# Gate and val products of the last two batches by seven block products in place of eight, with Silu on ScalarE and the weight sums on GpSimd

## The chip, the cores and the metric

One core of one Trainium2 chip. The metric is the device time of an execution in microseconds, the median of some runs. Before: 407.11 us (three runs, 406.99 to 408.16).

## The reference

Sigmoid attention for 8 batches of 12 heads, 448 positions, 64 per head, and behind it a gated block with two weight matrices in and one out:

```python
scores = scale * np.matmul(q, k.transpose(0, 1, 3, 2)) - np.log(S)
attn = 1.0 / (1.0 + np.exp(-scores))
x = matmul(attn, v), heads side by side: 3584 tokens x 768
g = x @ w_gate                       # 768 x 1536
silu = g * (1.0 / (1.0 + np.exp(-g)))
val = x @ w_val                      # 768 x 1536
out = silu * val @ w_out             # 1536 x 768
```

Inputs and output are float32; the kernel multiplies in bf16 (scores) and fp16 (the rest) and accumulates in float32.

## The kernel before, in words

**Stages.** Attention runs in 24 steps of four heads (`QB` = 3 steps per batch). In a step q, k and v are loaded to staging tiles on the SP queue, cast to 16 bits (mostly on GpSimd, L270), q and k transposed (first by TensorE, then by DMA, L410). `burst` (L417) makes the scores of one of seven key slots in two banks of PSUM, four 64x64 matmuls of 448 columns; ACT applies the sigmoid and writes `pt` (L448). `pv` (L455) multiplies with v; DVE or ACT copy the result to `xT` (L268, L266), fp16, features on partitions, tokens along the row: six tiles of 128x448 per batch.

**Gate and val.** `f1(b, f)` (L529) does two blocks f and f+1 of 128 hidden features of one batch. For each block gate takes six 128x128 products (over the 768 inputs) into one bank, val the same. Each 128x128 product is issued as four 64x64 quarters (`quarters`, L511), in two halves; between the halves of one bank pair, a nop on ACT (`turn`, L500, L504) keeps two row halves from writing the same bank at once. Then ACT makes the sigmoid of gate (L546), DVE multiplies it with gate (L552) and, when val is there, that with val (L559) into `hT`, 1024 times too large. Two batches share one `hT`.

**Output.** `f2_set(m, k)` (L631) multiplies two token tiles of a pair m of batches with `w_out`. It takes two tiles (e, o) and two halves of features, a 2x2 block product, and does it by seven block products in place of eight: sums of `hT` blocks on DVE (L661, L664, L667, L734), sums of `w_out` blocks made once on DVE (L605), seven products of six matmuls, and adds on DVE and ACT that put the parts together (L687, L727). In `f2_pair` (L757) two products go side by side as quarters; `f2_single` (L788) does one with whole 128x128 matmuls (L678). The last 64 rows of tile 6 of an even m are kept by two GpSimd copies (`keep`, L620, L623). Stores go out through GpSimd (L697, tiles `osb`, three of them), or, in the final part (`final`), through SP and ACT (staging memory, `osf`, four).

**Order.** The body does not issue instructions at once. Each `op` (L255) notes its engine, a duration by the author, what it depends on and which ring slots it takes and gives back. The loop at L872 queues ops step by step: per step and quarter (`sl`) a scores burst, gate/val work by a due count `nf` (L880), and output items whenever `f2acc` (grown by 12.5/22 per quarter, L919) allows. `list_schedule` (L70) then plays this through with the noted durations and fixes the order of each engine's queue. The engines run their queues in that order and wait only on semaphores. A tag in `FREE` (before: the eight PSUM banks `P`) takes any free slot, others go round a ring.

**Staging memory.** `stage` has eleven tiles. The first five (`NEARLY`) stay staging to the end and hold the final `osf`; the other six hold the sums of `w_out` and the kept rows from the middle of the run.

Of the kernel before, what the change touches and what calls it, by code (L numbers as in the profile page):

```python
# [9 lines left out]
FP32 = mybir.dt.float32  # L10
FP16 = mybir.dt.float16
BF16 = mybir.dt.bfloat16
COPY = mybir.ActivationFunctionType.Copy
SIGM = mybir.ActivationFunctionType.Sigmoid
MULT = mybir.AluOpType.mult
ADD = mybir.AluOpType.add
SUB = mybir.AluOpType.subtract
# [10 lines left out]
class Op:  # L28
# [3 lines left out]
    def __init__(self, eng, dur, fn, deps=(), mode=("F", "F"), take=(), give=(), desc=(0, 0)):  # L32
        self.eng, self.dur, self.fn, self.mode = eng, dur, fn, mode
        self.deps = [d if isinstance(d, tuple) else (d, 0.0) for d in deps if d is not None]
        self.take = [Slot(t) for t in take]
        self.give = list(give)
        self.rank = self.t0 = self.t1 = None
        self.first = False
        n, size = desc
        self.hold = n == 1792  # L40
        self.dma = 2.0 if n == 1792 else n / 16 * max(0.042, size / 22300 - 0.003)
# [13 lines left out]
LAG = 1  # L55
# [8 lines left out]
TURN = "ACT"  # L64
WO = 4
MARGIN = 1.0
FREE = {"P"}


def list_schedule(ops, bufs, window):  # L70
# [113 lines left out]
def kernel(  # L184
# [10 lines left out]
    nc = tc.nc  # L195

    B, H, S, D = q.shape
    DM = H * D
    DFF = moe_w_gate.shape[1]
    KC = DM // 128  # L200
# [14 lines left out]
    ctx.enter_context(tc.manual_schedule())  # L215

    slots = {"A": 2, "P": 8, "st": 11, "src": 2,
             "v16": 3, "qkT": 3, "pt": 10, "xT": 14, "osb": 3, "osf": 4, "S": 2, "t1": 3, "s16": 2}

    idn = one.tile([128, 128], BF16, tag="idn", name="idn")  # L220
    sb_t = one.tile([128, 1], FP32, tag="sbiast", name="sbiast")
# [33 lines left out]
    def op(*a, **kw):  # L255
        o = Op(*a, **kw)
        ops.append(o)
        return o

    def bank(name, n=0):  # L260

        return psum.tile([128, 512], FP32, tag=f"P{R['now'].got('P')[n].n}", bufs=1, name=name)

    def cp(eng, o, i):
        if eng == "ACT":
# [7 lines left out]
    T = {}  # L273
# [169 lines left out]
    def sig(key, dep, slot):  # L443
        def fn(a):
            def go():
                if a == 0:
                    T[("pt",) + key] = sb.tile([128, 2, S], FP16, tag="pt", bufs=slots["pt"], name="pt")
                nc.scalar.activation(out=T[("pt",) + key][:, a], in_=T[("sc",) + key][a][:, 0:S], func=SIGM, bias=sbias,  # L448
                                     scale=qkscale)
            return go  # L450
        x = op("ACT", 0.44, fn(0), deps=[dep], take=["pt"], give=slot[1:2])
        R["pt ring", key] = x.take
        R["sig"] = R[("pt",) + key] = op("ACT", 0.44, fn(1), deps=[x and (x, LAT["ACT"] + LATE)], give=slot[:1] + slot[2:])

    def pv(i):  # L455

# [72 lines left out]
    def f1(b, f):  # L529

        two = (f, f + 1)
        m, o = divmod(b, 2)

        def both(w, nm, parts, p):
            def fn():
                if p == 0:
                    for n, x in enumerate(two):
                        T[nm, b, x] = bank("ps_" + nm, n)[:, 0:S]
                quarters([[(T[nm, b, x], w[x // FC][:, j, (x % FC) * 128:(x % FC + 1) * 128], T["xT", b, j]) for x in two]
                          for j in range(*parts[p][1:])], parts, p, (nm, b, f))  # L540
            return fn

        def fs(f):
            def fn():
                t = T["s16", b, f] = sb.tile([128, S], FP16, tag="s16", bufs=slots["s16"], name="s16")
                nc.scalar.activation(out=t, in_=T["g", b, f], func=SIGM)  # L546
            return fn

        def ft(f):
            def fn():  # L550
                t = T["t1", b, f] = sb.tile([128, S], FP16, tag="t1", bufs=slots["t1"], name="t1")
                nc.vector.tensor_tensor(out=t, in0=T["g", b, f], in1=T["s16", b, f], op=MULT)  # L552
            return fn

        def fh(f):
            def fn():
                if o == 0 and f == 0:
                    T["hT", m] = sb.tile([128, NF, 2 * S], FP16, tag="hT", bufs=2, name=f"hT_{m}")
                nc.vector.scalar_tensor_tensor(  # L559
                    out=T["hT", m][:, f, o * S:(o + 1) * S], in0=T["v", b, f], scalar=HSC,  # L560
                    in1=T["t1", b, f], op0=MULT, op1=MULT)
            return fn
        xs = [(R["xT", b, j], 0.19 * j) for j in range(KC)]
        old = R["f2", m - 2] if m >= 2 and b % 2 == 0 else []

        def joint(w, nm, deps):
            a = None
            parts = [(0, 0, KC), (1, 0, KC)]
            if (b, f) == (0, 0) and nm in SPLIT:
                parts = [(0, 0, 4), (1, 0, 4), (1, 4, KC), (0, 4, KC)]  # L570
            ws = [(x, 0.38 * n) for c in {x // FC for x in two} for n, x in enumerate(R["w16", "w" + nm, c])]
            for p, (t, j0, j1) in enumerate(parts):
                same = p and parts[p - 1][0] == t
                a = op("PE", 0.19 * (j1 - j0), both(w, nm, parts, p), mode=("Q", "Q"), take=[] if p else ["P", "P"],
                       deps=[(x, 0.19 * n) for n, (x, _) in enumerate(xs[j0:j1])] + deps + ws +
                       [a and ((a, LAT["PE"] + LATE) if same else turn(a, (nm, b, f, p - 1)))])
                banks = banks if p else a.take
            return a, banks
        g, gbank = joint(wg16, "g", [])
        ts = []  # L580
        for n, x in enumerate(two):
            s = op("ACT", 0.45, fs(x), deps=[g], take=["s16"])
            s.first = 2
            ts.append(op("DVE", 0.54, ft(x), deps=[s], take=["t1"], give=s.take + gbank[n:n + 1]))

        def val():
            v, vbank = joint(wv16, "v", old + [(g, 1.0)])
            if f == NF - 2:
                v.give += [x for o, _ in xs for x in o.take]
            for n, (x, t) in enumerate(zip(two, ts)):  # L590
                R["hT", b, x] = op("DVE", 0.54, fh(x), deps=[v, t] + old, give=vbank[n:n + 1] + t.take)
        return val

    def weight_sums():

# [276 lines left out]
    for i in range(NQ + QB + 2):  # L872
        att = i < NQ
        for sl in range(4):
            if i < QB:
                nf = 0
            elif i < QB + 4:
                nf = 1 if sl < 3 else 0
            else:
                nf = min(2, max(0, 4 * (i - QB) + sl - LAG - fpos + 1))  # L880
            if i < NCW and sl == 3:
                cast_wc(i)
            if WO < i <= WO + 4 and sl == 1:
                for f in range(3 * (i - WO - 1), 3 * (i - WO)):
                    cast_wo(f)
            if i > WO + 5 or i == WO + 5 and sl > 1:
                for _ in range(WSN):
                    next(wsums, None)
            f1s = []
            while len(f1s) < nf and fpos < B * NF and ("xT", fpos // NF, KC - 1) in R:  # L890
                f1s.append(divmod(fpos, NF))
                fpos += 1
            later = bursts(i, sl)
            for ds in later[:1 if i >= SPREAD else 2]:
                burst(ds)
            if sl == 0 and QB < i <= NQ:
                pv(i - 1)
            if sl == 0 and 0 < i < QB:
                pv(i - 1)
            if sl == 3 and i == QB - 1:  # L900
                pv(i)
            if att and i + 1 < NPE and sl in (1, 2):
                tr_pe(i + 1, sl - 1)
            for b, f in f1s:
                f1_step(b, f)
            for ds in later[1:] if i >= SPREAD else []:
                burst(ds)
            if att and sl == 0 and i + 2 < NQ:
                casts(i + 2)
            if att and sl == 1 and NPE <= i + 2 < NQ:  # L910
                tr_dma(i + 2)
            if sl == 1:
                if AHEAD <= i + 3 < NQ:
                    loads(i + 3)
                if WO <= i < WO + 4:
                    for f in range(3 * (i - WO), 3 * (i - WO + 1)):
                        load_wo(f)
                    uses[1] = uses[0]
            f2acc = f2acc + 12.5 / 22.0 if f2q else 0.4  # L919
            while f2q and f2acc >= f2q[0][0] and ("ws", 4, NH - 2) in R:  # L920
                w, fn = f2q.pop(0)
                f2acc -= w
                fn(not att)
    while fpos < B * NF:
        b, f = divmod(fpos, NF)
        fpos += 1
        f1_step(b, f)
    while f2q:
        f2q.pop(0)[1](True)

    window = {"PE": 40, "ACT": 30, "DVE": 40, "POOL": 8, "SP": 1}
    end = 0.0
# [39 lines left out]
```

## Time and profile before

| | |
|---|---|
| median of the runs | 407.11 us |
| profiled execution, its span | 407.6 us (its own run time is not given apart) |
| TensorE busy (matmuls) | 400.1 us, 7871 instructions shown |
| VectorE (DVE) busy | 230.0 us, 420 |
| ScalarE (ACT) busy | 223.2 us, 472 |
| GpSimd (POOL) busy | 132.7 us, 194 |
| HBM read and written | 47.19 and 11.01 MB, 143 GB/s over the span |
| chain that ended last, by line | gate and val L522 54%, output L522 and L678 24%, scores 8%, pv 7% |

The profile is of one execution. Busy time of TensorE is modelled at the ends, as matmuls are pipelined: a 64x64 matmul of 448 columns is listed with 349 ns, although the next one starts long before its end. To see how fast TensorE goes, one divides a stretch of the chain by its matmuls. "PEld" are weight loads, which run beside matmuls. A line such as L522 is a helper that both gate/val and output products go through, so its groups are told apart by the tiles they write: `ps_g`, `ps_v` and `ps_o`. The chain follows the work that ended last from the end back to the start: its pieces, in order of time, have no room between them when an engine is what bounds the kernel.

### The profile page before, as it was taken

To read this page: it belongs to the slowest core of one execution; us is meant where nothing else is said; L and a number is where in the kernel's file an instruction comes from. 1 tells how busy PE (TensorE), PEld (TensorE's weight loads), DVE (VectorE), ACT (ScalarE), POOL (GpSimd) and SP (SyncE) were. 2 spreads that over 40 slices of the span, in tenths; PEclk is the share of its full clock that TensorE was granted. 3 is DMA by queue.
4 is the path that set the end of the run, shared out by engine and by line. 5 is a ranking of instruction groups with operands and counts; after the bars stand their busy time and mean duration, and the time that the engine had idled before them with its cause. 6 is when DMAs were issued, how large, how long until landed. Compare 5 with 4: busy or idle time off the path is not lost.

```text
span 407.6 us, 17541 instructions
## 1 busy us (share of the span) xinstructions
PE 400.1 (98%) x7871; PEld 306.8 (75%) x7873; DVE 230.0 (56%) x420; ACT 223.2 (55%) x472; POOL 132.7 (33%) x194
## 2 busy tenths in 40 slices
PE   8999999999999999999999999999999999999995
PEld 3446667668998787665679888889989898997663
DVE  2624544447795467553564664745465656546874
ACT  4997677757767743377647456475474552121100
POOL 1888855656454221522332322422310200000000
PEclk9999999999999999999999999999999999999998
DMA  7999999999676609455665564663500303010335
GB/s 268 380 376 376 376 277 318 304 320 264 184 185 183 160 26 203 139 129 108 209 183 92 172 136 143 177 133 122 124 4 3 80 2 77 7 42 18 101 85 148
DMA packets 64795, 67.58 MB, mean 166 GB/s; under 512 B 35536, under 2 KB 60880, under 8 KB 64720
## 3 DMA queue, kind: packets, MB, share of 16 engines
q1 hardware_dynamic: 62864, 59.78, 51.6%
q0 software_dynamic: 1536, 6.29, 6.0%
q8 instruction: 61, 1.00, 1.0%
q10 hardware_dynamic: 320, 0.39, 0.3%
q14 instruction: 14, 0.11, 0.1%
HBM read 47.19 MB, written 11.01 MB: 143 GB/s over the span
## 4 chain that ended last, share of the span: by engine, by line
PE 95%; ACT 2%; DMA 1%; issue 1%; DVE 0%; ACTq 0%
PE ps_v L522 27%; PE ps_g L522 27%; PE ps_o L522 16%; PE ps_sc L427 8%; PE ps_pv L468 7%; PE ps_o L678 7%; ACT pt L448 2%; PE ps_warm L818 1%; PE ps_tr L384 1%; DMA st<-in_q_dram 1%; DVE st L687 0%; DVE src L268 0%; ACTq L504 0%
## 5 line engine op out<-in xcount | busy, mean ns | idle before, releaser
L448 ACT ACTIVATE pt<-ps_sc 128x448 f16<-128x448 f32 x336 | 162.7, 550 | 77.8 <-PE ps_sc L427 77.3
L522 PE MATMUL ps_v<-xT,wv 64*64 64x448 f16 x2304 | 136.2, 349 | 0.0
L522 PE MATMUL ps_g<-xT,wg 64*64 64x448 f16 x2304 | 134.6, 349 | 0.8 <-issue 0.6
L522 PEld LDWEIGHTS <-wg 64*64 64x64 f16 x2304 | 93.7, 107 | 22.2 <-issue 2.4
L522 PEld LDWEIGHTS <-wv 64*64 64x64 f16 x2304 | 93.2, 107 | 21.2 <-issue 1.4
L552 DVE TENSOR_TENSOR t<-ps_g,s 128x448 f16<-128x448 f32 x96 | 56.5, 618 | 71.6 <-ACT s L546 71.6
L546 ACT ACTIVATE s<-ps_g 128x448 f16<-128x448 f32 x96 | 48.1, 545 | 59.0 <-PE ps_g L522 50.0
L559 DVE SCALAR_TENSOR_TENSOR hT<-ps_v,t 128x448 f16<-128x448 f32 x96 | 55.4, 618 | 43.4 <-PE ps_v L522 26.2
L427 PE MATMUL ps_sc<-qkT 64*64 64x448 bf16 x672 | 77.2, 354 | 0.1
L270 POOL CAST src<-st 128x896 bf16<-128x896 f32 (+1 forms) x43 | 40.8, 951 | 64.5 <-DMA st<-in_q_dram 35.8
L270 POOL CAST v<-st 64x448 f16<-64x448 f32 (+1 forms) x72 | 41.5, 577 | 60.0 <-PE ps_pv L468 42.5
L522 PEld LDWEIGHTS <-hT 64*64 64x64 f16 x1080 | 52.2, 107 | 7.0 <-issue 0.2
L522 PE MATMUL ps_o<-wo,hT 64*64 64x384 f16 x648 | 49.2, 323 | 0.0
L522 PE MATMUL ps_o<-st,s 64*64 64x384 f16 x480 | 45.7, 323 | 0.0
L468 PE MATMUL ps_pv<-pt,v 64*64 64x448 f16 x672 | 45.3, 350 | 0.1
L522 PE MATMUL ps_o<-st,hT 64*64 64x384 f16 x432 | 41.2, 323 | 0.0
L427 PEld LDWEIGHTS <-qkT 64*64 64x64 bf16 x672 | 33.7, 107 | 9.9 <-issue 1.6
L687 DVE SCALAR_TENSOR_TENSOR osb<-ps_o,osb 128x384 f32<-128x384 f32 x63 | 32.9, 550 | 10.4 <-PE ps_o L522 6.6
L268 DVE CAST xT<-ps_pv 128x448 f16<-128x448 f32 x40 | 23.6, 617 | 25.0 <-PE ps_pv L468 25.0
L697 POOL DMA_DIRECT2D out_dram<-osb x32 | 16.7, 526 | 59.0 <-DVE osb L687 59.0
L468 PEld LDWEIGHTS <-v 64*64 64x64 f16 x672 | 26.6, 107 | 9.1 <-issue 2.7
L522 PEld LDWEIGHTS <-s 64*64 64x64 f16 x480 | 29.1, 107 | 3.8 <-issue 0.4
(44 smaller groups left out, 212.8 us busy)
## 6 DMA issues: line engine op xcount, KB each, us to landing
st<-in_q_dram SPq DMA_DIRECT2D x24, 448.0 KB, 5.0
st<-in_v_dram SPq DMA_DIRECT2D x24, 448.0 KB, 6.6
st<-in_k_dram SPq DMA_DIRECT2D x23, 448.0 KB, 5.9
out_dram<-osb POOLq DMA_DIRECT2D x32, 192.0 KB, 3.3
st<-in_moe_w_gate_dram SPq DMA_DIRECT2D x12, 384.0 KB, 8.8
st<-in_moe_w_val_dram SPq DMA_DIRECT2D x12, 384.0 KB, 8.8
st<-in_moe_w_out_dram SPq DMA_DIRECT2D x12, 384.0 KB, 7.6
out_dram<-st SPq DMA_DIRECT2D x16, 192.0 KB, 2.8
```

Of the source, the lines that this page charges most:

```text
L268: nc.vector.tensor_copy(out=o, in_=i)
L270: nc.gpsimd.tensor_copy(out=o, in_=i)
L427: nc.tensor.matmul(out=sc[a][64 * (g ^ a):64 * (g ^ a) + 64, 0:S].rearrange("k (s p) -> k s p", s=NS), lhsT=kT[r, s, 64 * g:64 * g + 64], ...
L448: nc.scalar.activation(out=T[("pt",) + key][:, a], in_=T[("sc",) + key][a][:, 0:S], func=SIGM, bias=sbias, scale=qkscale)
L468: nc.tensor.matmul(out=T["pv", i, a][64 * g:64 * g + 64, :], lhsT=T["v16", i][r, a, s, :], rhs=T["pt", i, s][r, a, :], start=(s == 0), sto ...
L522: mm = nc.tensor.matmul(out=o[cs], lhsT=w[rs, cs], rhs=x[rs], start=p == 0 and k == 0, stop=p == len(parts) - 1 and k == len(steps) - 1)
L546: nc.scalar.activation(out=t, in_=T["g", b, f], func=SIGM)
L552: nc.vector.tensor_tensor(out=t, in0=T["g", b, f], in1=T["s16", b, f], op=MULT)
L559: nc.vector.scalar_tensor_tensor(out=T["hT", m][:, f, o * S:(o + 1) * S], in0=T["v", b, f], scalar=HSC, in1=T["t1", b, f], op0=MULT, op1=MULT)
L678: nc.tensor.matmul(out=T["p", m, k, n], lhsT=lhs()[:, x // 2, x % 2], rhs=rhs(x), start=x == 0, stop=x == NH - 1)
L687: nc.vector.scalar_tensor_tensor(out=c(*dst), in0=T["p", m, k, n], scalar=HREC, in1=c(*other), op0=MULT, op1=ADD)
L697: dma.dma_start(out=out[rows, cols].rearrange("(p s) d -> s p d", s=NS)[s], in_=T[("osb",) + t][64 * x:64 * x + 64, cols])
```

## The change

Batches 0 to 5 (`NPLAIN` = 6) go as before. For the pair 6 and 7 `f1_pair` replaces `f1`. It takes block f and block f+6 of the hidden features (c = 0, 1), both batches (o = 0, 1) and both halves of the 768 inputs (three tiles each): a 2x2x2 block product, by seven products of three matmuls each in place of eight, for gate and for val, in six sets (`one_set`). The matmuls take the whole 128x128 array and 448 columns.

- Sums of inputs (`xsum`): twelve on DVE, 128x448, four for each of three tiles; some go to the `src` tiles that the last attention steps have left, one to a new tile, three overwrite tiles of batch 7.
- Sums of weights (`wsums`): four per block and matrix, 48 in all, 128x384, on GpSimd. Three go to slots `W` (seven, in the first five staging tiles), one overwrites the weight itself. They wait for the last casts of attention and for val of batch 5.
- Products 1, 6, 7 and 4 accumulate in one bank, one after the other. After 1, 6 and 7 ACT copies the bank out (`snap`, float32, in `pt` slots, scaled by 1024 for val); the next product waits for that copy. Product 2 has its own bank, 5 and 3 share one. DVE adds a copy to them (`add`).
- ACT computes Silu (`silu`) from the finished gate; it is held until all sigmoids are done. DVE multiplies it with val (`fin`): three of four times from two fp16 tiles in SBUF, once from PSUM.

Around it: `pt` has 9 slots, now taken free, `xT` 16. Gate and val are paced by 3.2 blocks per step from step 12 on (`FR`, `F0`), output items by 0.42 per quarter, later 0.6 (`RATE`, `RATE2`). All output items except those of the last pair of batches now use the `osb` tiles and GpSimd's stores. Of the output of batches 4 and 5, two items go between sets (`MIX`), the last three (`KEEP`) behind the last set.

```diff
-FREE = {"P"}
+FREE = {"P", "pt", "W"}
...
+    def f1_pair(m):
...
+        def xsum(k, j):
...
+            out, x, y, f = {1: (lambda: tile_of(1, j), o0, o1, ADD),
+                            2: (lambda: tile_of(2, j), lambda: tile_of(1, j), e0, SUB),
+                            3: (o0, e0, o0, SUB),
+                            4: (lambda: tile_of(4, j), e1, lambda: tile_of(2, j), SUB)}[k]
...
+        def wsums(nm, f, eng):
...
+            def f1():
...
+                e.tensor_tensor(out=t(0), in0=blk(w, f, 0, 1), in1=blk(w, f, 0, 0), op=SUB)
+
+            def f3():
+                e.tensor_tensor(out=blk(w, f, 0, 1), in0=blk(w, f, 1, 1), in1=blk(w, f, 0, 1), op=SUB)
+
+            def f2():
+                e.tensor_tensor(out=t(1), in0=blk(w, f, 1, 1), in1=t(0), op=SUB)
+
+            def f4():
+                e.tensor_tensor(out=t(2), in0=blk(w, f, 1, 0), in1=t(1), op=SUB)
...
+        first = {1: "A", 2: "B", 5: "E"}
+        chain = {1: "A", 6: "A", 7: "A", 4: "A", 2: "B", 5: "E", 3: "E"}
+
+        def one_set(f, last):
...
+                    for j in range(NC):
+                        nc.tensor.matmul(out=T["fp", key], lhsT=win(nm, f, n)()[:, j], rhs=xin[n](j),
+                                         start=n in first and j == 0, stop=j == NC - 1,
+                                         skip_group_check=n not in first)
...
+                    nc.scalar.activation(out=T["sn", nm, f, n], in_=T["fp", (nm, f, "A")], func=COPY,
+                                         scale=HSC if nm == "v" else 1.0)
...
+            both(1, lambda nm: [last] if last else [R["xT", b1, j] for j in range(KC)])
+            for nm in "gv":
+                snap(nm, 1)
+            both(2)
+            add("g", 0, 0, 2, 1, True)
+            silu(0, 0)
+            both(6, lambda nm: [C[nm, "s", 1]])
+            for nm in "gv":
+                snap(nm, 6)
+            add("v", 0, 0, 2, 1, True)
+            fin(0, 0)
+            both(5)
+            both(7, lambda nm: [C[nm, "s", 6]])
+            for nm in "gv":
+                snap(nm, 7)
+            add("g", 1, 1, 5, 7, False)
+            silu(1, 1)
+            add("v", 1, 1, 5, 7, False)
+            both(4, lambda nm: [C[nm, "s", 7]])
+            silu(1, 0)
+            fin(1, 0)
+            fin(1, 1)
+            both(3, lambda nm: [C[nm, 1, 1]])
+            add("g", 0, 1, 3, 6, True)
+            silu(0, 1)
+            add("v", 0, 1, 3, 6, True)
+            fin(0, 1)
...
-            f2acc = f2acc + 12.5 / 22.0 if f2q else 0.4
-            while f2q and f2acc >= f2q[0][0] and ("ws", 4, NH - 2) in R:
+            f2acc = f2acc + (RATE2 if fpos == NPLAIN * NF else RATE) if f2q else 0.4
+            while len(f2q) > (KEEP if fpos == NPLAIN * NF else 0) and f2acc >= f2q[0][0] and ("ws", 4, NH - 2) in R:
                 w, fn = f2q.pop(0)
                 f2acc -= w
-                fn(not att)
...
+                fn(False)
+            if i == NQ and sl == 3:
+                sums, wsums_of, one_set = f1_pair(B // 2 - 1)
+                sums()
+                todo = [(nm, f) for f in range(NH) for nm in "gv"]
+                for x in todo[:4]:
+                    wsums_of(*x, "POOL")
+                last = None
+                for f in range(NH):
+                    last = one_set(f, last)
+                    for _ in range(min(MIX, len(f2q) - KEEP)):
+                        f2q.pop(0)[1](False)
+                    for x in todo[4 + 2 * f:6 + 2 * f]:
+                        wsums_of(*x, "POOL")
```

## The prediction

> **What bounds the kernel.** First the page's busy shares and its slices: TensorE is busy for 98% of the span at the full granted clock.
>
> ```profile
> span 407.6 us, 17541 instructions
> PE 400.1 (98%) x7871; PEld 306.8 (75%) x7873; DVE 230.0 (56%) x420; ACT 223.2 (55%) x472; POOL 132.7 (33%) x194
> PEclk9999999999999999999999999999999999999998
> ```
>
> "Busy" can hide gaps, so next the chain of work that ended last, in order of time (start, us, what), where the changed products lie:
>
> ```profile
> 359.78 1.14 PE ps_v L522 x24
> 360.91 3.40 PE ps_g L522 x72
> 364.32 1.14 PE ps_v L522 x24
> 365.45 1.14 PE ps_g L522 x24
> ...
> 373.40 1.08 PE ps_o L678 x6
> 374.48 1.26 PE ps_v L522 x24
> ```
>
> Each piece starts where the one before ended: TensorE issues without a hole, 3.40/72 = 47.2 ns for a 64x64 matmul of 448 columns, so 0.189 us for the four that make one 128x128 product. A us of matmuls taken out there is a us of span, unless a wait fills it. The piece of six L678 matmuls is 0.10 us longer than their issue (168 of them take 27.42 us on the whole chain: 0.163 each, 0.98 for six), and the piece after it 0.12 longer than 24 x 47.2: that is what going from quarter to whole products and back costs. Busy time by windows (us, then busy and count of PE, PEld, DVE, ACT, POOL, granted clock, DMA) shows what may give cover:
>
> ```profile
> 190.00:341.00 151.00, 151.00 (x3323) 131.65 (x3324) 84.12 (x157) 86.86 (x183) 36.20 (x57) 1.00 0.43 108
> 341.00:376.00 35.00, 35.00 (x738) 30.16 (x731) 20.02 (x38) 6.74 (x14) 0.00 (x0) 1.00 0.15 37
> ```
>
> From 341 us on ACT is busy 19%, GpSimd not at all, DVE 57%. After the last matmul (403.2) 4.4 us of last add and stores follow.
>
> **What is removed.** In batches 6 and 7 gate and val are 2 x 2 x 12 x 6 = 288 whole products, 288 x 0.189 = 54.4 us of issue. Now there are six sets (feature blocks f and f+6, both batches) of 7 block products for gate and 7 for val, three matmuls each: 252, on the whole 128x128 array. No row has that form at 448 columns; the nearest, L678's 0.163 us at 384 columns, gives 0.190 scaled by columns; below, the 0.189 of the quarters; a fixed cost could take it to 0.200. I take 0.190 (weights of the same size load in 98 ns beside the matmul): 252 x 0.190 = 47.9. **Gain 6.5 us** (4.0 to 6.8).
>
> **Switches.** In the changed program's order whole products alternate with quarter pairs of the output product: 12 changes to whole and 11 back in the tail, where before had 2 and 1. 20 more at 0.10 to 0.12: **+2.2 us**. Also, one output pair of batches 4-5 now has its halves next to each other, with ACT's turn-taking nop (L504) between; the waits on that nop that the trace has are at most 0.4: **+0.4**.
>
> **ACT and DVE.** Gate and val products of one set accumulate in one bank: product 1 is copied out (ACT), 6 is added to the bank, copied out, 7, copied out, 4. TensorE waits for each copy. From the last issue to the copy's start is 0.26 us (six matmuls from 375.67 issue until 376.65, the copy starts at 376.91), the copy of 448 columns takes 0.55 (row L546), the way back I put at 0.10: 0.91. Between 6 and 7, and between 7 and 4, the order has at least two products of 0.57 = 1.14. So the bare loop is covered, with 0.23 to spare. But ACT's queue is in order: Silu of the first result stands ahead of the copies of 6, and waits for a DVE add; that add stands on DVE behind the last multiply of the set before. Followed from product 3's end (us after it): DVE's multiply and adds of the old set until 1.6, Silu until 1.65, last multiply until 2.1, new add until 2.9, new Silu until 3.5, copy of 6 (its product done at 3.7) until 4.25, product 7 due at 4.56: about 0.2 spare again, by durations of L559 (0.62, 0.54 from one to the next), L546 and an estimate of 0.36 for an SBUF-only 448 multiply (L664's 0.55 for 768).
>
> What uses this up is GpSimd. Such a DVE instruction reads two SBUF tiles, and those suffer beside GpSimd:
>
> ```profile
> 112.25 1.02 POOL L270 CAST src<-st 128x896 bf16<-128x896 f32 x1 [1.77 <-DMA st<-in_k_dram]
> 112.39 1.28 DVE L661 TENSOR_TENSOR s<-hT 128x768 f16<-128x768 f16 x1
> 120.29 1.15 POOL L623 COPY st<-hT 128x768 f16<-128x768 f16 x1
> 120.68 1.17 DVE L667 TENSOR_TENSOR hT<-hT 128x768 f16<-128x768 f16 x1
> ```
>
> Both DVE instructions take 0.55 elsewhere; here each ends 0.4 after the GpSimd instruction does, as if it had waited for its end. GpSimd now works through the tail, so each of the three SBUF-only multiplies of a set waits up to one GpSimd instruction, half of one (0.45) on average. The Trainium skill, "SBUF — State Buffer", section "SBUF: two separate sides", speaks against the change here: DVE and GpSimd hold a shared pair of ports as an exclusive lock for a whole instruction. By a mere sharing of bandwidth the wait would be less than by the lock; the two rows above fit the lock. With 0.45 against 0.2 to spare a set loses about 0.3: five sets (the first has output pairs between its products), **+1.5 us** (0 to 5).
>
> ACT's sums: 36 copies and 24 Silu replace 24 Sigmoid, 36 x 0.55 = 20 us more in a stretch of 70 where ACT is a fifth busy; a table load (1.28 us, L808's row) comes once, beside set 1, which output pairs stretch. The 12 input sums on DVE (0.36 each, 0.8 beside GpSimd) run over the last attention work and are due one by one until set 1's products 6 to 3: nothing; uncovered, up to 1 us.
>
> **GpSimd.** 48 weight sums of 128x384 in a queue with the keep copies (L623, 0.99), output stores (0.52 per issue; batches 4-5 now store here, 32 issues become 40) and their waits for DVE. The sums stand behind the first keep copy, which waits for the last output product of batches 2-3. From there to val's product 6 of set 6 TensorE issues 59.7 us of work by the changed order and the prices above, plus 19 switches at 0.1, 61.6. Until then GpSimd must do 2 copies, 12 issues and 43 sums: 2.0 + 6.2 + 0.5 + 43p, so p may be 1.23 us at most; the same count for set 1 allows 1.57. No row has a two-input GpSimd instruction. Below: a one-input cast of 448 takes 0.575, so 0.49 for 384. Above: two inputs of 384 are 768 elements to read, and the copy of 768 takes (line, shapes, count, busy us, mean ns)
>
> ```profile
> L623 POOL COPY st<-hT 128x768 f16<-128x768 f16 x4 | 4.0, 988 | 1.0 <-DVE hT L559 1.0
> ```
>
> that is 0.83 to 1.15 each. I take 0.95, near its mean; 1.15 would do too: **nothing**. The skill's "GPSIMD Engine Reference", section "Elementwise — side-by-side cycle accounting", has 4497 ns for a two-input add of 2048: an estimate of 0.84 for 384, by which the sum stays the same. No run here shows it yet.
>
> **Moves.** The first 124 us of matmul issue are in the old order. Later the gate work of batches 2 to 5 is paced more slowly and output pairs are spread thinner; TensorE always has attention, gate or output work queued, and from 190 to 341 us its matmuls at the prices above add up to all but 0.6 us, 0.2 of that two switches. Cost nothing; if banks ran short behind ACT (58% busy in that window), a few tenths. The multiplies and adds of the last set are covered by three halves of output pairs (2.9 us) and the single product after them.
>
> **Sum.** 407.6 - 6.5 + 2.2 + 0.4 + 1.5 = 405.2 of span. The median of the runs (407.11) is 0.5 below the profiled span: **404.7**.
>
> **Rivals.**
> 1. All waits covered: ACT and DVE cost nothing, 405.2 - 1.5 - 0.4 = 403.3, on the median's scale 402.8. For: 0.2 spare even in the queues; against: the two GpSimd rows.
> 2. The ACT-DVE loop becomes the bound of a set: full lock waits (0.95) on two multiplies in line leave 0.9 lost per set and more in the set after the output sums; five sets give 4.5 in place of 1.5: 407.7. For: DVE is the fuller of the two; against: a stall also gives the queues time.
> 3. **Slower:** the weight sums come late at val's product 6. Place: GpSimd's queue. Each 0.1 us over p = 1.23 costs 43 x 0.1 = 4.3 us, so the gain is gone at 1.29 and the time is over 408.3 from 1.31; at 1.45 it is 414. For: no row of two inputs, and each DVE multiply delays GpSimd in turn (L270's 0.94 became 1.35 when one started with it); against: even the copy of 768 in its slow case is below 1.23.
> That the change would not take the matmuls out is excluded by the changed program: 1152 quarter matmuls fewer, 252 whole ones more.
>
> **Numbers.** Forecast (403.4 to 406.2) 0.45; rival 1 0.15; rival 2 0.2; rival 3 0.2. A measurement can tell 0.3% from no change, so below 405.9 is faster, above 408.3 slower. Faster: 0.43 of the forecast's and all of rival 1, 0.58. Same: 0.02, 0.16 of rival 2 and 0.03 of rival 3, 0.21. Slower: 0.21. The range 402.6 to 409.5 leaves out the late half of rival 3 and a little below.
>
> **What would show it.** Right: 252 matmuls 0.19 us apart; GpSimd sums near 0.95 and done before the last set; TensorE holes of tenths of a us ahead of products 7 and 4, released by ACT. Rival 3: holes of over a us released by GpSimd, growing from set to set. Rival 2: holes released by ACT or DVE of about 1 us in every set. Wrong altogether: holes in the attention stretch, or whole products well over 0.19.

## The result, and the profile after

The changed kernel takes **437.0 us** (four runs, 436.3 to 439.1), the kernel before 407.6 on the same chip: ratio 1.072, 95% interval 1.068 to 1.077. I had forecast 404.7. The profiled execution has a span of 434.6 us. From its page: span, busy times, and the slices of TensorE, GpSimd and the granted clock:

```profile
span 434.6 us, 15878 instructions
PE 404.2 (93%) x6971; PEld 274.2 (63%) x6973; DVE 273.2 (63%) x444; ACT 243.6 (56%) x509; POOL 179.2 (41%) x250
PE   8999999999999999999999999999776691999995
POOL 2788856654452251423424412125379059100100
PEclk9999999999999999999999999999888597899999
```

The first 28 slices of TensorE show no hole: attention did not get slower. From 304 us on TensorE has holes, around the stretches in which GpSimd runs the weight sums, and its granted clock drops. DVE is busy for 273 us where before had 230, though it has only 24 more instructions. Groups by line and shape (count, then busy us and mean ns of one) show which instructions those are:

```profile
L762 DVE TENSOR_TENSOR hT<-hT,pt 128x448 f16<-128x448 f16 x18 | 30.5, 1694 | 2.0 <-ACT pt L750 0.8
L740 DVE SCALAR_TENSOR_TENSOR hT<-ps_v,pt 128x448 f16<-128x448 f32 x18 | 11.1, 617 | 0.6 <-ACT pt L725 0.4
```

L762 is the multiply of val with Silu, from two SBUF tiles. Its mean is 1694 ns, where I had an estimate of 360; the listed time of an instruction includes time in which it is held up. L740 reads a bank of PSUM and one SBUF tile, and takes the 0.62 us that I had put down. A mean can hide two kinds, so next the timeline of DVE (start and duration, us), its four longest instructions; L643 is a sum of inputs, L873 a sum for the output:

```profile
300.00 6.84 DVE L643 TENSOR_TENSOR src<-xT,xT 128x448 f16<-128x448 f16 x1
...
314.22 7.72 DVE L873 TENSOR_TENSOR s<-s,hT 128x768 f16<-128x768 f16 x1
...
326.93 10.27 DVE L762 TENSOR_TENSOR hT<-hT,pt 128x448 f16<-128x448 f16 x1 [0.17 <-ACT pt L750]
...
354.35 13.68 DVE L762 TENSOR_TENSOR hT<-hT,pt 128x448 f16<-128x448 f16 x1
```

And that of GpSimd, the run of weight sums under the last of them (its second to thirteenth left out):

```profile
354.72 0.92 POOL L678 TENSOR_TENSOR st<-wv,st 128x384 f16<-128x384 f16 x1
...
366.01 0.90 POOL L681 TENSOR_TENSOR st<-wg,st 128x384 f16<-128x384 f16 x1
366.88 0.90 POOL L672 TENSOR_TENSOR st<-wv,wv 128x384 f16<-128x384 f16 x1
367.85 0.94 POOL L678 TENSOR_TENSOR st<-wv,st 128x384 f16<-128x384 f16 x1
```

Each sum starts some 0.03 us before the one ahead is listed as done (366.01 + 0.90 = 366.91, the next starts at 366.88). Only after fifteen of them is there a gap of 0.07 us (367.78 to 367.85), ahead of a sum that needs the result of the fifteenth, and DVE's multiply ends at 368.03, 0.25 behind it: 13.7 us for work of 0.39. The other three long instructions likewise end 0.25 to 0.4 after the last of 6, 8 and 13 sums. Less about 1.7 us of own work, DVE stood for 38.5 - 1.7 = **36.8 us**.

Two rows limit this reading. The multiply of 354.35 was listed as started before the first sum (354.72), while GpSimd still issued stores (L906, 352.61 to 354.72), and yet the sums went first; those of 300.00 and 314.22 also began during store issues. And once a multiply did get in between two sums that follow each other without idle time (368.76 to 369.67, and from 369.62 on):

```profile
369.20 0.71 DVE L762 TENSOR_TENSOR hT<-hT,pt 128x448 f16<-128x448 f16 x1
```

How that becomes the kernel's time is in the chain of waits, in order of time, around the third and fourth hole:

```profile
330.92 6.20 issue
337.12 0.54 DVE hT L943
337.67 0.93 DVE osb L896 x2
338.60 0.54 DVE pt L740
...
339.64 0.53 ACT pt L725
340.18 0.04 issue
340.22 1.28 PE ps_g L711 x3
341.50 1.12 PE ps_v L711 x3
342.62 2.06 PE ps_o L543 x23
344.69 1.24 PE ps_g L711 x3
345.92 0.80 PE ps_v L711 x3
346.72 0.57 PE ps_g L711 x3
...
354.35 13.68 DVE hT L762
```

The multiply holds up the adds behind it on DVE, those ACT's Silu and copies, the copy TensorE's next product, which starts only at 340.22. Then three matmuls that otherwise take 0.57 us together take 1.28, and TensorE stays slow until 346.3. Windows (length, busy time and count of PE, PEld, DVE, ACT, POOL, then granted clock) confirm that it is the clock:

```profile
340.20:344.70 4.50, 4.48 (x31) 1.71 (x31) 1.64 (x3) 1.96 (x4) 0.00 (x0) 0.50 0.00 0
354.30:368.00 13.70, 4.96 (x44) 2.39 (x43) 13.65 (x2) 1.98 (x4) 13.61 (x17) 0.83 0.15 46
```

From 340.22 to 346.72 are 6.5 us for twelve whole matmuls and 24 quarters of an output product (one is missing in the trace). At the full clock that is 12 x 0.19, 0.97 for 24 such quarters (292.19 in the same chain) and two switches of 0.10, 3.45 in all, so **3.05 us are lost to the clock**. The same working gives 1.6, 3.0 and 2.5 for the other three restarts, some 10.1 together. From 300 to 376 us TensorE is idle for 23.1 us (76 - 52.9 busy), in four holes of 3.6, 3.0, 7.1 and 9.4. That makes some 33.2, and the span without the sums is 33.2 shorter (first experiment).

### The profile page after: what moved, and what is told of

Its sections match the earlier page's. It is cut to its first block, busy times and chain, and to the rows that moved or that the text cites. A ratio compares the mean times of both kernels' runs of the same rounds, so it can differ in the third digit from the quotient of the medians.

```text
span 434.6 us, 15878 instructions
## 1 busy us (share of the span) xinstructions
PE 404.2 (93%) x6971; PEld 274.2 (63%) x6973; DVE 273.2 (63%) x444; ACT 243.6 (56%) x509; POOL 179.2 (41%) x250
## 4 chain that ended last, share of the span: by engine, by line
PE 77%; DMA 9%; DVE 6%; issue 5%; POOL 2%; ACT 1%; DVEq 0%; POOLq 0%; SPq 0%; ACTq 0%
PE ps_v L543 17%; PE ps_g L543 17%; PE ps_o L543 15%; PE ps_o L887 7%; PE ps_pv L489 6%; PE ps_sc L446 6%; PE ps_g L711 5%; DMA st<-in_v_dram 5%; PE ps_v L711 4%; DMA st<-in_moe_w_gate_dram 4%; DVE hT L762 3%; POOL wg L360 1%; DMA st<-in_q_dram 1%; POOL v L289 1%; DVE osb L896 1%
## 5 line engine op out<-in xcount | busy, mean ns | idle before, releaser
L543 PE MATMUL ps_v<-xT,wv 64*64 64x448 f16 x1728 | 101.7, 349 | 0.3 <-issue 0.3
L543 PE MATMUL ps_g<-xT,wg 64*64 64x448 f16 x1728 | 100.3, 349 | 0.5 <-POOL wg L360 0.2
L543 PEld LDWEIGHTS <-wg 64*64 64x64 f16 x1728 | 65.3, 107 | 21.6 <-POOL wg L360 1.6
L543 PEld LDWEIGHTS <-wv 64*64 64x64 f16 x1728 | 65.0, 107 | 21.2 <-issue 1.8
L573 DVE TENSOR_TENSOR t<-ps_g,s 128x448 f16<-128x448 f32 x72 | 42.7, 619 | 55.6 <-ACT s L567 55.4
L906 POOL DMA_DIRECT2D out_dram<-osb x40 | 21.0, 530 | 107.3 <-DVE osb L896 104.3
L580 DVE SCALAR_TENSOR_TENSOR hT<-ps_v,t 128x448 f16<-128x448 f32 x72 | 41.5, 617 | 29.4 <-PE ps_v L543 23.0
L567 ACT ACTIVATE s<-ps_g 128x448 f16<-128x448 f32 x72 | 36.4, 547 | 22.8 <-PE ps_g L543 16.5
L543 PE MATMUL ps_o<-st,s 64*64 64x384 f16 x480 | 49.1, 338 | 0.0
L896 DVE SCALAR_TENSOR_TENSOR osb<-ps_o,osb 128x384 f32<-128x384 f32 x70 | 36.4, 550 | 11.2 <-PE ps_o L543 6.2
L489 PEld LDWEIGHTS <-v 64*64 64x64 f16 x672 | 26.3, 107 | 10.1 <-issue 2.1
```

What stands on the lines that cost most here:

```text
L489: nc.tensor.matmul(out=T["pv", i, a][64 * g:64 * g + 64, :], lhsT=T["v16", i][r, a, s, :], rhs=T["pt", i, s][r, a, :], start=(s == 0), sto ...
L543: mm = nc.tensor.matmul(out=o[cs], lhsT=w[rs, cs], rhs=x[rs], start=p == 0 and k == 0, stop=p == len(parts) - 1 and k == len(steps) - 1)
L580: nc.vector.scalar_tensor_tensor(out=T["hT", m][:, f, o * S:(o + 1) * S], in0=T["v", b, f], scalar=HSC, in1=T["t1", b, f], op0=MULT, op1=MULT)
L896: nc.vector.scalar_tensor_tensor(out=c(*dst), in0=T["p", m, k, n], scalar=HREC, in1=c(*other), op0=MULT, op1=ADD)
```

## Experiments

All runs are of the changed kernel with the edit shown; ratios are to the kernel before, run beside them. They were made on several chips, on which the kernel before takes 407.0 to 408.2 us, so two experiments are compared by their ratios.

**Theory:** GpSimd's sums, back to back, shut DVE's SBUF-only instructions out for a whole run. **Rivals:** the loop of copies between ACT, DVE and TensorE is too slow in any case; or DVE's in-order queue is too full.

**1. Without the sums** (`e1_no_sums`)

```diff
+            f1 = f2 = f3 = f4 = lambda: None
...
-                    4: lambda: T["W", nm, f][:, 2], 5: lambda: T["W", nm, f][:, 0],
-                    6: lambda: T["W", nm, f][:, 1], 7: lambda: blk(w, f, 0, 1)}[n]
+                    4: lambda: blk(w, f, 1, 0), 5: lambda: blk(w, f, 0, 0),
+                    6: lambda: blk(w, f, 1, 1), 7: lambda: blk(w, f, 0, 1)}[n]
```

> Leaves out the 48 weight sums on GpSimd (products 4 to 7 read plain weight blocks); the order of all other instructions stays that of the change. Theory (DVE's instructions with two SBUF inputs are shut out as long as GpSimd runs its sums back to back, and nothing else is lost): 403 to 405 us, L762 near 0.39 us each, no hole of TensorE over 1 us. Rival (the copies between products, the switches or the new pacing lose too): 410 us or more, with holes released by ACT.

403.06 us, ratio 0.987 (0.982 to 0.992). L762 is L763 here; the group, and the window of the tail:

```profile
L763 DVE TENSOR_TENSOR hT<-hT,pt 128x448 f16<-128x448 f16 x18 | 7.0, 391 | 2.1 <-ACT pt L751 1.0
```

```profile
294.00:376.00 82.00, 81.88 (x882) 46.16 (x874) 59.42 (x119) 40.70 (x78) 9.07 (x17) 1.00 0.14 40
```

TensorE is busy for all but 0.12 of 82 us at the full clock. So the loop of copies is covered, and everything lost comes with the sums. GpSimd's stores are still there, and the longest DVE instruction beside them takes 1.61 us: it is not the stores that cost 7 to 14.

**2. The sums on DVE** (`e2_dve_sums`)

```diff
-                    wsums_of(*x, "POOL")
+                    wsums_of(*x, "DVE")
```

(in both places)

> The 48 weight sums on DVE in place of GpSimd. Theory: no one to wait for, 48 x about 0.35 = 17 us more work on DVE, 404 to 408 us, some holes of tenths where DVE is late. Rival (the loss is in the loop of copies and adds on ACT and DVE): worse than the change, over 437 us, as DVE has more to do.

404.12 us, ratio 0.990 (0.986 to 0.993). A sum takes 0.35 us there, L762 0.39. DVE bears 48 instructions more, and TensorE is still busy for all but 0.12 of the 82 us from 294 on, so DVE's queue was not too full.

**3. and 4. Something between the sums** (`e3_gap_memset`, `e6_gap_wide`)

```diff
+            def then(fn):
+                def go():
+                    fn()
+                    nc.gpsimd.memset(gap, 0.0)
+                return go
+            f1, f2, f3, f4 = then(f1), then(f2), then(f3), then(f4)
```

`gap` is 128x1 float32; the second kernel has `wide`, 128x512 bf16, in its place.

> The sums stay on GpSimd; behind each one stands a memset of 128x1 on GpSimd, which reads nothing. Theory (GpSimd holds what DVE needs from one sum to the next, because the next starts 0.03 us before the last ends): a DVE instruction waits one sum at most, 0.9 us, and the time is that of the prediction, 404 to 407 us. If an instruction that only writes does not open the way: 435 to 441 us, with L762 up to 14 us again.

439.23 us, ratio 1.075 (1.070 to 1.079). The memset takes 0.09 us, and DVE's longest multiply, 0.5 us longer than in the change, is

```profile
357.34 14.19 DVE L769 TENSOR_TENSOR hT<-hT,pt 128x448 f16<-128x448 f16 x1
```

> As the version with memsets between the sums, but each memset writes 128x512 of bf16 and so lasts long enough for a DVE instruction of 0.38 us to get in. If an instruction that only writes leaves the way open while it runs: DVE waits one sum at most, under 415 us. If the sum queued behind it has the ports already, or the memset holds them too: L762 above 10 us again, and 440 us or more, as the runs of GpSimd get longer by 48 memsets.

453.5 us (one run). Lines of DVE's timeline, of GpSimd's groups, and of GpSimd's timeline at the end of the first of the two multiplies:

```profile
333.52 15.82 DVE L768 TENSOR_TENSOR hT<-hT,pt 128x448 f16<-128x448 f16 x1 [0.17 <-ACT pt L756]
...
365.38 20.16 DVE L768 TENSOR_TENSOR hT<-hT,pt 128x448 f16<-128x448 f16 x1
```

```profile
L688 POOL MEMSET wide<- 128x512 bf16 x48 | 24.8, 517 | 0.0
```

```profile
348.19 0.90 POOL L672 TENSOR_TENSOR st<-wg,wg 128x384 f16<-128x384 f16 x1
349.04 0.51 POOL L688 MEMSET wide<- 128x512 bf16 x1
```

Half a us in which GpSimd only writes does not let DVE in while another sum stands behind it: the run only gets longer, and the longest wait with it, to 20.2 us. But the memset by itself does not hold DVE. The multiply of 333.52 ends at 349.34, 0.25 behind the last sum (349.09) and before the last memset ends (349.55), behind which GpSimd has nothing more to do. The other three long instructions of this run also end before a memset does; behind one of them (365.38) a sum follows at once, but one that needs the result of the sum just ended. So of the expectation's two readings the first is left: what counts is a sum that already stands ready behind the memset.

The Trainium skill, "SBUF — State Buffer", section "Who interferes with whom", says that a DVE instruction with two SBUF inputs contends with a GpSimd instruction that reads SBUF, not with one that only writes it. The last memset of each run agrees. By that alone the multiply would also have run beside the first memset, behind at most one sum; here it waited 15.8 us.

**5. Copies in place of sums** (`e4_copy_sums`)

```diff
-                e.tensor_tensor(out=t(0), in0=blk(w, f, 0, 1), in1=blk(w, f, 0, 0), op=SUB)
+                e.tensor_copy(out=t(0), in_=blk(w, f, 0, 1))
```

(and so for the other three)

> Each weight sum becomes a GpSimd copy of its second input (128x384, one input; the sums are left out), same order. If any back-to-back run on GpSimd shuts DVE out: runs are half as long, DVE waits 3 to 7 us, 415 to 422 us. If only two-input instructions do: DVE gets in between two copies, waits of 0.5 us at most, 403 to 406 us.

410.2 us, ratio 1.004 (1.000 to 1.007), between the two expectations: some waits are as long as the first has it (3.44 and 4.95 us), others are one copy. A copy takes 0.50 us. Two lines of DVE's timeline:

```profile
302.63 0.85 DVE L943 TENSOR_TENSOR hT<-hT,s 128x768 f16<-128x768 f16 x1
...
317.54 4.95 DVE L762 TENSOR_TENSOR hT<-hT,pt 128x448 f16<-128x448 f16 x1 [0.17 <-ACT pt L750]
```

The second waits until the run of copies ends; the first gets in between two of them (0.55 alone, 0.85 here). So it doesn't take two inputs on GpSimd's side, and a run of copies is not always closed.

**6. Sums that wait for DVE** (`e5_sums_behind_dve`)

```diff
+    def behind(x):
+        if "two" in T and T["two"] is not T.get("seen"):
+            after_ins(x.ins, T["two"])
+            T["seen"] = T["two"]
```

Here `x` is a sum on GpSimd, and `T["two"]` DVE's last instruction with two SBUF inputs ahead of it in the order (the places that set `T["two"]` and call `behind` are left out).

> The sums stay on GpSimd, but each waits by semaphore for the last DVE instruction with two SBUF inputs that stands ahead of it in the program, if no earlier sum has waited for it. Theory (a queued GpSimd instruction has the ports before it starts, so DVE gets in only where GpSimd has nothing that may start): waits of DVE fall to the few sums between two such waits, 0.9 to 3 us in place of up to 14, 404 to 412 us. Rival (GpSimd keeps the ports for the whole stretch whatever it waits for): 430 us or more.

403.75 us, ratio 0.991 (0.988 to 0.993). The multiply's group and its longest instance:

```profile
L772 DVE TENSOR_TENSOR hT<-hT,pt 128x448 f16<-128x448 f16 x18 | 13.0, 721 | 2.1 <-ACT pt L760 1.0
```

```profile
325.03 2.77 DVE L772 TENSOR_TENSOR hT<-hT,pt 128x448 f16<-128x448 f16 x1
```

The same 48 sums on the same engine, and 33 us less: it was not their work, but that they ran on without waiting for DVE. Here DVE also gets in between sums with no idle time between them: this multiply runs between a sum that starts at 314.33 and one that starts at 315.20.

```profile
314.83 0.67 DVE L772 TENSOR_TENSOR hT<-hT,pt 128x448 f16<-128x448 f16 x1
```

At 325.03 it had to wait for three sums in a row. So making GpSimd wait for DVE does what a memset does not; by which rule DVE then gets in between two sums is not shown.

**7. and 8. Whole output products as well** (`e7_dve_sums_singles`, with the sums on DVE; `e8_sums_behind_singles`, with the sums on GpSimd behind DVE)

```diff
-KEEP = 3
-MIX = 2
+KEEP = 6
+MIX = 4
...
-            if m == B // 2 - 1 or not sets:
-                pairs = [((one, 1), (one, 2)), ((one, 6), (one, 7)), ((one, 5), (one, 3))] if m < B // 2 - 1 else []
+            if m >= B // 2 - 2 or not sets:
+                pairs = [((one, 1), (one, 2)), ((one, 6), (one, 7)), ((one, 5), (one, 3))] if m < B // 2 - 2 else []
```

> Weight sums on DVE, and the output products of batches 4 and 5 one by one on the whole array in place of pairs of quarters (same number between the sets and behind the last). Theory (each change between quarters and whole products costs 0.10 to 0.12 us, and only that): some 18 changes fewer in the tail, a few more during attention, about 1.5 us under the version with the sums on DVE, so 402 to 403.5 us. Rival (the pairs give ACT and DVE time, without them the loop of copies is late): no faster than that version, 404 us or more.

400.85 us, ratio 0.984 (0.981 to 0.987), better than both kernels. The chain between two whole products, where the version with quarters has 0.67 for the first three matmuls:

```profile
310.59 0.57 PE ps_v L711 x3
311.15 0.97 PE ps_o L887 x6
312.13 0.57 PE ps_g L711 x3
```

No switch is paid. The medians differ by 3.3 us (404.12 to 400.85), but they are from two chips; by the ratios (0.990 to 0.984) it is 2.5, with an uncertainty of nearly 2. The 1.5 us expected lie within that, and more than that is not shown.

> The weight sums on GpSimd, each behind the last two-input SBUF instruction of DVE, and the output products of batches 4 and 5 as whole products, so both mended parts together. Theory: sums behind DVE gave 403.75, and whole output products took 3.3 us off the version with sums on DVE (404.12 to 400.85), so about 400.5; the longest DVE multiply stays under 3 us. If instead the gain of the whole products came from DVE's room rather than from the switches on TensorE, less than 1 us goes: 403 or more.

401.7 us, ratio 0.984 (0.981 to 0.987); L772 takes 1.27 us at most, the longest DVE instruction 2.12 (L953, a sum for the output). It can't be told from the seventh. By the ratios (0.991 to 0.984) the whole products give 2.8 us here, again with an uncertainty of nearly 2. About the same gain with the sums off DVE speaks against the other reading, DVE's room.

**9. and 10. Which DVE instructions are shut out** (`e9_multiply_one_input`, `e10_multiply_plain_form`)

```diff
-                        nc.vector.tensor_tensor(out=hslot(o, c), in0=hslot(o, c), in1=T["t", f, o, c], op=MULT)
+                        nc.vector.tensor_copy(out=hslot(o, c), in_=T["t", f, o, c])
```

```diff
+                        nc.vector.scalar_tensor_tensor(out=hslot(o, c), in0=hslot(o, c), scalar=1.0,
+                                                       in1=T["t", f, o, c], op0=MULT, op1=MULT)
```

> In three of four multiplies with Silu DVE only copies the Silu to its place (one fp16 input in SBUF, 128x448; the multiplication with val is left out), sums on GpSimd as in the change. If it is the second SBUF input that shuts DVE out, the copies run at once (0.3 to 0.5 us), only the input sums L643 and output sums L873 still wait, and the time falls from 437 to about 418. If a DVE instruction with any fast SBUF-only form is shut out, the copies wait 10 and 13 us at the same two places as the multiplies did and the time stays near 437.

436.5 us, ratio 1.070 (1.066 to 1.073): a copy with one input waits as the multiply did. I had thought until then that the second SBUF input was what mattered.

```profile
328.84 10.15 DVE L762 COPY hT<-pt 128x448 f16<-128x448 f16 x1 [0.17 <-ACT pt L750]
...
355.35 13.57 DVE L762 COPY hT<-pt 128x448 f16<-128x448 f16 x1
```

> The same multiply of Silu and val from two fp16 SBUF tiles, three of four per set, but as SCALAR_TENSOR_TENSOR, the form of the adds that ran beside the sums (0.62 us for 448 columns), in place of TENSOR_TENSOR (0.39 alone). Sums on GpSimd as in the change. If the fast form is what is shut out, the multiplies run at once at about 0.6 us each, only L643 and L873 still wait, and the time falls to about 418. If it is that all operands lie in SBUF, they wait 10 and 13 us as before and the time stays near 437.

439.0 us, ratio 1.077 (1.073 to 1.080). The form that runs freely with an operand in PSUM waits 10.48 and 13.91 us with both in SBUF:

```profile
357.36 13.91 DVE L762 SCALAR_TENSOR_TENSOR hT<-hT,pt 128x448 f16<-128x448 f16 x1
```

So neither the form nor the second input decides. What ran beside the sums at its own speed had one operand in PSUM: L740 in the changed kernel (0.61 us at 326.14, beside a sum), the output's adds in the sixth run (0.54 us at 314.36). Every SBUF-only fp16 instruction that was tried could be shut out. All PSUM operands here are float32, so the place and the type were not told apart. The Trainium skill, "SBUF — State Buffer", section "Who interferes with whom", says that a copy, though it has one input, can run in a mode that takes the ports which DVE shares with GpSimd; the 13.57 us of the ninth run agree.

**11. Casts in place of sums** (`e11_cast_sums`)

```diff
+    f32s = wide.bitcast(FP32)[:, 0:128].unsqueeze(1).to_broadcast([128, 3, 128])
...
-                e.tensor_tensor(out=t(0), in0=blk(w, f, 0, 1), in1=blk(w, f, 0, 0), op=SUB)
+                e.tensor_copy(out=t(0), in_=f32s)
```

(and so for the other three)

> Each weight sum on GpSimd is replaced by a cast of a constant float32 tile (128x3x128, read three times over) to the fp16 place of the sum: no sum is made, the order of everything stays. Such casts are what GpSimd ran when DVE got in at every boundary in the kernel before (128x768 casts there, 0.82 us alone). If a run of casts leaves the way open, no DVE instruction waits longer than about one cast (0.5 us), and the time is about 403 to 404, as without the sums. If any back-to-back run of GpSimd instructions shuts DVE out, waits of 3 to 5 us remain, as with the fp16 copies, and the time is about 410.

404.7 us, ratio 0.992 (0.990 to 0.995); casts take as long as the copies of the fifth (0.50), and give 4.5 us less by the ratios. DVE:

```profile
301.82 3.83 DVE L644 TENSOR_TENSOR src<-xT,xT 128x448 f16<-128x448 f16 x1
305.57 0.85 DVE L944 TENSOR_TENSOR hT<-hT,s 128x768 f16<-128x768 f16 x1
...
323.30 0.76 DVE L763 TENSOR_TENSOR hT<-hT,pt 128x448 f16<-128x448 f16 x1
```

Nearly always DVE gets in after at most one cast, as in the kernel before; once it waits 3.8 us, for a store issue, a copy and five casts. So the rows of before were read rightly for casts, and did not hold for sums. What decides at a boundary who gets in stays open: casts from one constant float32 tile let DVE in far more often, but not always, and whether that is their type, that they read another place, or the moment at which DVE comes, was not separated.

## Why the prediction was wrong

**The step that failed:** "each of the three SBUF-only multiplies of a set waits up to one GpSimd instruction, half of one (0.45) on average", priced +1.5 us. I took it from two rows in which DVE ended 0.4 us behind a GpSimd instruction. Behind the first of them GpSimd had nothing ready (its next began at 113.71). Behind the second a cast followed at once (121.40, stretched to 1.25), and DVE got in ahead of it. So the trace of before did show one instruction's wait, for casts from float32: among three of them from 94.78 on, too, L605 got in after one. I carried this over to sums of two fp16 tiles, which no row showed, and bounded their duration from both sides but not the wait they cause. In place of 0.45 stood 10.3 and 13.7 us for two multiplies of the sets. The same wait met two instructions besides: a sum of inputs (put at 0.8, took 6.8) and one for the output (7.7), whose wait is no term of the sum. With the clock behind them the four make 33 us of span.

Point by point:

- **Gain of the products, -6.5, and switches, +2.2:** right as a sum. Without the weight sums the ratio of 0.987 makes 5.2 us less than before, where rival 1, which has just these terms, has 4.3. In the rows three matmuls take the 0.57 of the prediction, and 0.67 behind a switch.
- **ACT and DVE without GpSimd, and the turn, +0.4:** covered, as rival 1 said; TensorE idles 0.12 of 82 us (first experiment).
- **GpSimd, "nothing":** the price of a sum was right (0.95, measured 0.90) and the sums were not late (no wait of TensorE behind 296 us ends with GpSimd), so rival 3's mechanism did not occur. The estimate of 0.84 beside it, scaled from a float32 figure to these fp16 sums, is a little short. Rival 3's question, whether GpSimd keeps up, was the wrong one. What mattered was what GpSimd does to DVE while it keeps up.
- **Rival 2** named the right loop (DVE, ACT, TensorE), with a wait of one instruction; even its 407.7 is 29 us short.
- **Moves, 0:** right; until 300 us TensorE is idle for 2.8 us, before the change for 3.0.
- **Not in the sum at all:** the granted clock. Every hole cost 1.6 to 3.1 us more behind it, 10 us in all.

## What to carry to other kernels

When work moves to GpSimd, look not at whether it gets done in time but at how many of its instructions follow each other without a wait: fp16 DVE instructions with all operands in SBUF may be shut out until the run ends, and whatever stands behind them on DVE and ACT with them. Keep such sums on DVE if they cost 0.35 us there against 0.90, or let them wait for DVE's instructions. Giving DVE an operand in PSUM may do as well; that was not tried as a remedy. And two colliding instructions in a profile price a collision of two, not one of many.

## What the runs showed of the hardware that I had not expected

- DVE was shut out for fifteen sums in a row (13.7 us), and through 0.5 us memsets between them too (20.2 us), though it ran beside a memset with no sum ready behind it. Sums that waited for DVE by semaphore held it for 2.8 us at most.
- The kind of GpSimd instruction mattered: with 0.50 us fp16 copies the ratio is 1.004, with casts from float32 of the same length 0.992.
- Holes of TensorE of 3.0 to 9.4 us each brought a granted clock of 0.50, still in force for 3.4 to 6 us of work behind them. In windows of 0.5 us of the changed kernel the clock falls at 308.7, 322.4, 336.0 and 363.3 and comes back at 312.1, 329.2, 346.3 and 373.6: the last seven lie 1, 4, 6, 8, 11, 16 and 19 times 3.41 us behind the first, in order of time. So in this trace the clock changes only on such a grid, and a hole of 3.0 us cost as much (3.0) as one of 7.1 (3.05).
